# Windowed attention with sink keys before a routed expert: the attention rebuilt around cast loads, key blocks and packed sinks

## The chip, the cores and the metric

The kernel runs on 1 core of one Trainium2 chip. The metric is the device time of one execution in microseconds, the median of the runs; lower is better. The profile is one execution taken by the hardware profiler. PE is TensorE's matmul side and PEld its weight loads; DVE is VectorE, ACT ScalarE, POOL GpSimd, SP SyncE.

## The reference

Four batches, eight heads, 768 positions, head size 64. Each query sees the first four keys (the sinks) and the last 128 keys up to itself:

```
scores = (q @ k.T) / 8;  keep = (key < 4) | (0 <= query - key < 128)
a = softmax(where(keep, scores, -1e9));  x = a @ v          # heads side by side: x is [4, 768, 512]
```

Then, for each batch, a routed expert works on the 128 rows of x with the highest score:

```
s = x @ w_gate;  top = the 128 rows with the largest s
out = x;  out[top] += sigmoid(s[top]) * (relu(x[top] @ w1) @ w2)     # w1 is 512 x 1024, w2 1024 x 512
```

## The kernel before

The work goes batch by batch, and in a batch by six query blocks of 128. A framework takes the program's operations and sets the order on each engine when the kernel is built; the engines then work through fixed lists, and each instruction waits for the semaphores that its operands need. Score tiles turn through two PSUM banks, value tiles through three, everything of the expert through three more.

`prep` (L111 to L169) loads q, k and v of a batch in float32 by SP's queue in 256 KB pieces, whose rows are 256 bytes long (L120, L124, L129), and the four sink rows of v (L134). DVE and ACT cast q and k to bf16 (L139, L140), TensorE transposes two heads at a time (L149), and DVE copies the results out: keys as 128 rows that hold two heads (`KT`, L160), queries into `QTz`, where the rows of the other head are zero (L155, L157, the zeros by POOL at L143). So one score matmul uses all 128 rows of the array though a head has 64.

`stage_scores` makes, per query block, head and visible key block, a 128x128 score tile (L193), adds the mask by a matmul of an identity with a mask of 512 columns (L195) and takes the exponential on ACT (L198). From block 2 on a third set of score matmuls against key block 0 serves the sinks (L209, L213). `stage_av` multiplies the exponentials (as weights, float32) by v: 128 moving columns per head, of which 64 are v, one is a column of ones that gives the softmax's sum, and the rest is not used (L227); the sinks need another matmul per head with a `vsk` that is zero outside four rows (L231). DVE divides (L237, L238), computes the row's routing score (L243), a diagonal of it (`dg`, L249), and a float32 matmul with ones spreads it over all partitions (L253, L260).

`moe_gen` is the expert of the batch before, run in pieces between the query blocks: DVE ranks the rows by counting larger scores (`cjunk`, L283), makes a one-hot matrix per 128 rows (`E`, L286) and its transpose (`ET`), TensorE gathers (L298), multiplies by w1 (L315) and w2 (L322), scatters (L328); DVE adds x (`o_sb`, L331), and SP stores. The last batch's expert has nothing beside it.

Of the kernel before, what the change touches and what calls it, by code (L numbers as in the profile page):

```python
# [9 lines left out]
FP32 = mybir.dt.float32  # L10
# [4 lines left out]
B = 4  # L15
H = 8
# [6 lines left out]
CAP = 128  # L23
MASK_NEG = -30000.0
VSTRIDE = 66
VWIDTH = H * VSTRIDE + 62
# [3 lines left out]
def kernel(  # L30
# [17 lines left out]
    qk32 = ctx.enter_context(tc.tile_pool(name="qk32", bufs=1))  # L48
    vpool = ctx.enter_context(tc.tile_pool(name="vpool", bufs=2))
    qkb = ctx.enter_context(tc.tile_pool(name="qkb", bufs=1))  # L50
    tpool = ctx.enter_context(tc.tile_pool(name="tpool", bufs=2))
    ptpool = ctx.enter_context(tc.tile_pool(name="ptpool", bufs=2))
    xnpool = ctx.enter_context(tc.tile_pool(name="xnpool", bufs=2))
    opool = ctx.enter_context(tc.tile_pool(name="opool", bufs=3))
    mpool = ctx.enter_context(tc.tile_pool(name="mpool", bufs=1))
    spool = ctx.enter_context(tc.tile_pool(name="spool", bufs=2))
# [20 lines left out]
    nc.vector.tensor_copy(maskA0[:], maskB_f[:])  # L77
    maskD_f = cp.tile([128, 128], FP32, name="maskD_f", tag="maskD_f")
    nc.gpsimd.memset(maskD_f[:], 0.0)
    nc.gpsimd.affine_select(  # L80
        out=maskD_f[:], in_=maskD_f[:], compare_op=ALU.is_ge,
        fill=MASK_NEG, base=-1, pattern=[[-1, 128]], channel_multiplier=1,
    )
    maskD = cp.tile([128, 128], BF16, name="maskD", tag="maskD")
    nc.vector.tensor_copy(maskD[:], maskD_f[:])
    nc.gpsimd.memset(maskD_f[0:4, :], 0.0)
    maskC = cp.tile([128, 128], BF16, name="maskC", tag="maskC")
    nc.vector.tensor_copy(maskC[:], maskD_f[:])

    mask4 = {}  # L90
    for mname, mt in (("A0", maskA0), ("B", maskB), ("C", maskC), ("D", maskD)):
        m4 = cp.tile([128, 4, 128], BF16, name=f"mask4{mname}", tag=f"mask4{mname}")
        nc.vector.tensor_copy(out=m4[:, :, :], in_=mt[:, :].unsqueeze(1).to_broadcast((128, 4, 128)))  # L93
        mask4[mname] = m4
# [5 lines left out]

    wgb = cp.tile([128, DM], FP32, name="wgb", tag="wgb")
    nc.gpsimd.dma_start(out=wgb[:], in_=moe_w_gate.partition_broadcast(128))

    ones_f = cp.tile([128, 128], FP32, name="ones_f", tag="ones_f")
    nc.gpsimd.memset(ones_f[:], 1.0)


    class BatchState:
        pass

    def prep(b, first):  # L111
        st = BatchState()
        st.b = b
        qf = qk32.tile([128, NB, H, D], FP32, name="qf", tag="qf")
        kf = qk32.tile([128, NB, H, D], FP32, name="kf", tag="kf")
        vn = vpool.tile([128, NB, VWIDTH], FP32, name="vn", tag="vn")
        nc.gpsimd.memset(vn[:, :, :], 1.0)  # L117
        for c in range(NB):
            tsl = slice(c * 128, (c + 1) * 128)
            nc.sync.dma_start(out=qf[:, c, :, :],  # L120
                              in_=q[b, :, tsl, :].rearrange("h p d -> p h d"))
        for c in range(NB):
            tsl = slice(c * 128, (c + 1) * 128)
            nc.sync.dma_start(out=kf[:, c, :, :],  # L124
                              in_=k[b, :, tsl, :].rearrange("h p d -> p h d"))
        for c in range(NB):
            tsl = slice(c * 128, (c + 1) * 128)
            vdst = vn[:, c, 0:H * VSTRIDE].rearrange("p (h cc) -> p h cc", cc=VSTRIDE)[:, :, 0:D]
            nc.sync.dma_start(out=vdst, in_=v[b, :, tsl, :].rearrange("h p d -> p h d"))  # L129
        vsk = vpool.tile([128, H, 128], FP32, name="vsk", tag="vsk")  # L130
        nc.gpsimd.memset(vsk[:, :, :], 0.0)
        nc.gpsimd.memset(vsk[0:4, :, D:D + 1], 1.0)
        for h in range(H):
            nc.sync.dma_start(out=vsk[0:4, h, 0:D], in_=v[b, h, 0:4, :])  # L134

        qb = qkb.tile([128, NB, H, D], BF16, name="qb", tag="qb")
        kb = qkb.tile([128, NB, H, D], BF16, name="kb", tag="kb")
# [264 lines left out]
```

## Time and profile before

| | |
|---|---|
| runs | 286.36, 287.98, 288.23 us (median 287.98) |
| profiled execution, first to last instruction | 286.7 us |
| PE busy | 224.2 us (78%), 2096 matmul records |
| PEld busy | 194.5 us (68%) |
| DVE busy | 159.2 us (56%) |
| ACT busy | 107.9 us (38%) |
| POOL busy | 41.4 us (14%) |
| chain that ended last | PE 59%, DVE 30%, ACT 4%, DMA 3% |
| DMA | 27.88 MB in 80262 packets, 75568 of them under 512 bytes |

The profile gives the span of one execution; what lies around it is not in it, and the median stands 1.3 us above the span. A busy matmul engine is not one at its peak, since the records of neighbouring matmuls overlap: the distance from one start to the next tells more than the length of a record. A float32 matmul is two records (two passes), each with its own weight load.

### The profile page before, as it was taken

The numbers are of one execution on the slowest core, as the hardware profiler recorded it, in microseconds if no ns is written. First come the engines' busy times: TensorE is split into PE (matmuls) and PEld (weight loads), VectorE is DVE, ScalarE is ACT, GpSimd is POOL, SyncE is SP. The second block draws the span as 40 slices with busy tenths as digits, with TensorE's granted clock in tenths as the row PEclk, the third lists the DMA queues.
The fourth block names the chain that finished last, engine by engine and source line by source line (L and its number), as shares of the span: only waits on it lengthen the run. The fifth ranks groups of instructions, "written<-read, shape, count | busy, mean of one in ns | idle before, by whom it ended". The sixth has DMA issues, their size and how long they took to land.

```text
span 286.7 us, 5137 instructions
## 1 busy us (share of the span) xinstructions
PE 224.2 (78%) x2096; PEld 194.5 (68%) x2096; DVE 159.2 (56%) x366; ACT 107.9 (38%) x205; POOL 41.4 (14%) x33
## 2 busy tenths in 40 slices
PE   0100389948998889999976999999969999997671
PEld 0000268926898779889973799899838899994350
DVE  0799853484039498742469557233695332158814
ACT  0050037042752472376343431851534534424040
POOL 3599200000015500000650000000000000000000
PEclk9999999975999999999999899999997999999597
DMA  7999989979901097910024620000005000000415
GB/s 162 217 219 196 193 159 194 221 134 229 172 0 33 15 213 159 228 21 2 0 59 91 220 77 0 2 2 0 2 11 211 2 0 2 2 0 2 171 49 220
DMA packets 80262, 27.88 MB, mean 97 GB/s; under 512 B 75568, under 2 KB 76592, under 8 KB 80240
## 3 DMA queue, kind: packets, MB, share of 16 engines
q1 hardware_dynamic: 78592, 25.21, 41.5%
q0 software_dynamic: 1648, 2.36, 4.5%
q8 instruction: 16, 0.26, 0.4%
q14 instruction: 6, 0.05, 0.1%
HBM read 23.36 MB, written 6.29 MB: 103 GB/s over the span
## 4 chain that ended last, share of the span: by engine, by line
PE 59%; DVE 30%; ACT 4%; DMA 3%; issue 2%; SPq 0%; ACTq 0%; DVEq 0%
PE xg L227 25%; PE xg L231 9%; DVE cjunk L283 7%; PE sc L193 6%; PE sc L195 5%; PE trp L149 4%; DVE maskA L77 4%; DVE mask4D L93 3%; PE sk L209 3%; ACT pt L198 3%; DMA qf<-in_q_dram 2%; DVE qb L139 2%; DVE junk L243 2%; DVE o_sb L331 2%; DVE E L286 2%
## 5 line engine op out<-in xcount | busy, mean ns | idle before, releaser
L227 PE MATMUL xg<-vn,pt 128*128 128x128 f32 x704 | 110.4, 281 | 0.0
L227 PEld LDWEIGHTS xg<-vn,pt 128*128 128x128 f32 x704 | 96.7, 195 | 1.6 <-issue 0.6
L198 ACT ACTIVATE pt<-sc 128x512 f32<-128x512 f32 x88 | 50.1, 596 | 77.4 <-PE sc L195 76.8
L237 DVE RECIPROCAL rz<-xg 128x4 f32<-128x4 f32 x48 | 8.7, 182 | 93.9 <-PE xg L231 73.4
L231 PE MATMUL xg<-vsk,psk 128*128 128x128 f32 x256 | 50.1, 278 | 0.0
L193 PEld LDWEIGHTS <-KT 128*128 128x128 bf16 x352 | 28.5, 102 | 17.1 <-issue 13.2
L231 PEld LDWEIGHTS xg<-vsk,psk 128*128 128x128 f32 x256 | 39.6, 192 | 0.3
L193 PE MATMUL sc<-QTz,KT 128*128 128x128 bf16 x352 | 36.5, 227 | 1.8 <-ACT pt L198 0.9
L149 PE MATMUL trp<-ident_b,qb 128*128 128x128 bf16 x96 | 9.9, 253 | 34.6 <-DVE qb L139 21.8
L247 ACT CAST xb<-xn 128x512 bf16<-128x512 f32 x24 | 14.8, 616 | 56.5 <-DVE xn L238 56.5
L143 POOL MEMSET QTz<- 128x6144 bf16 x4 | 20.9, 5222 | 89.9 <-PE sk L209 89.9
L149 PEld LDWEIGHTS <-qb 128*128 128x128 bf16 x96 | 7.3, 112 | 36.1 <-DVE qb L139 32.1
L283 DVE TENSOR_SCALAR_CACHE_REDUCE cjunk<-sbc,scol 128x768 f32<-128x768 f32 x24 | 24.2, 1007 | 2.3 <-ACT sbc L263 2.3
L238 DVE TENSOR_TENSOR xn<-xg,rz 128x256 f32<-128x256 f32 x48 | 20.3, 423 | 2.2
L331 DVE TENSOR_TENSOR o_sb<-ops,xb 128x512 f32<-128x512 f32 x24 | 15.7, 682 | 6.6 <-PE ops L328 4.6
L213 ACT ACTIVATE psk<-sk 128x512 f32<-128x512 f32 x32 | 18.2, 599 | 0.5 <-PE sk L209 0.2
L328 PE MATMUL ops<-gye,ET 128*128 128x512 bf16 x24 | 9.3, 443 | 10.1 <-DVE o_sb L331 8.6
L243 DVE CUSTOM_DVE_ANT_0 junk<-xn,wgb 128x512 f32<-128x512 f32 x24 | 16.5, 686 | 0.4
L195 PE MATMUL sc<-mask4B,ident_b 128*128 128x512 bf16 x40 | 16.2, 404 | 0.0
L139 DVE TENSOR_SCALAR qb<-qf 128x1536 bf16<-128x1536 f32 x8 | 10.7, 1338 | 8.9 <-DMA qf<-in_q_dram 8.9
L117 POOL MEMSET vn<- 128x3540 f32 x4 | 12.2, 3052 | 9.3 <-PE xg L227 9.3
L209 PE MATMUL sk<-QTz,KT 128*128 128x128 bf16 x128 | 12.3, 218 | 0.5
(70 smaller groups left out, 255.3 us busy)
## 6 DMA issues: line engine op xcount, KB each, us to landing
qf<-in_q_dram SPq DMA_DIRECT2D x24, 256.0 KB
kf<-in_k_dram SPq DMA_DIRECT2D x24, 256.0 KB
vn<-in_v_dram SPq DMA_DIRECT2D x24, 256.0 KB
out_dram<-o_sb SPq DMA_DIRECT2D x24, 256.0 KB
w_sb<-in_moe_w_dram POOLq DMA_DIRECT2D x2, 1024.0 KB, 12.4
vsk<-in_v_dram SPq DMA_DIRECT2D x32, 1.0 KB
wgb<-in_moe_w_gate_dram POOLq DMA_DIRECT2D x1, 256.0 KB, 5.8
```

What stands on the lines that cost most here:

```text
L143: nc.gpsimd.memset(QTz[:, :, :], 0.0)
L149: nc.tensor.transpose(out=trp[:, c, :], in_=src[:, c, 2 * hp:2 * hp + 2, :], identity=ident_b[:],)
L193: nc.tensor.matmul(out=sc[:, hh, :], lhsT=kt_ap, rhs=qblk, start=(hh == 0), stop=False)
L195: nc.tensor.matmul(out=sc[:, :, :], lhsT=ident_b[:, :], rhs=m4[:, :, :], start=False, stop=True)
L198: nc.scalar.activation(out=pt[:, quad * 4:quad * 4 + 4, :], in_=sc[:, :, :], func=ACT.Exp)
L209: nc.tensor.matmul(out=sk[:, hh, :], lhsT=st.KT[:, hpi, 0:128], rhs=qblk, start=True, stop=True)
L227: nc.tensor.matmul(out=xg[:, hh, :], lhsT=pt_tiles[ci][:, h, :], rhs=vap, start=(ci == 0), stop=(ci == nterm - 1))
L231: nc.tensor.matmul(out=xg[:, hh, :], lhsT=psk[:, h, :], rhs=st.vsk[:, h, :], start=False, stop=True)
L238: nc.vector.tensor_tensor(out=xn32[:, g * 4:(g + 1) * 4, :], in0=xg[:, :, 0:D], in1=rz[:, :, :].to_broadcast((128, 4, D)), op=ALU.mult)
L243: nc.vector.tensor_tensor_reduce(out=junk[:, :], in0=xn_flat, in1=wgb[:, :], scale=1.0, scalar=0.0, op0=ALU.mult, op1=ALU.add, accum_out=s ...
L283: nc.vector.tensor_scalar(out=cjunk[:, :], in0=sbc[:, :], scalar1=scol[:, c:c + 1], scalar2=0.0, op0=ALU.is_gt, op1=ALU.add, accum_out=ran ...
L331: nc.vector.tensor_tensor(out=o_sb[:, :], in0=ops[:, :], in1=xb16[:, c, :], op=ALU.add)
```

## The change

q and k are loaded by POOL's queue and cast to bf16 on the way, with a position's number split as 6 x p + c, so that a partition gets six neighbouring rows of 64 numbers, 1536 bytes in DRAM. Batch 0 comes in four parts each of two heads, later batches in one piece for q and one for k. The transposes take one head at a time (a 64-column tile of the array), and the copies out of PSUM put the positions back in order: keys by DVE, queries by ACT. The zero-padded queries and their zeros are gone.

Scores are made per key block: one matmul of 64 array rows covers a head's key block and the 256 queries that see it (its own block and the next). Only key block 0 keeps the added mask, over four matmuls of 512 columns per batch. For the other blocks POOL zeroes the triangles in the exponentials with two `affine_select` of 128x512 per half of the heads, 18 per batch and 72 in all. The sinks of all heads are packed into one 128-row weight (`ksk`), 32 rows of scores and one matmul per half with v's sink rows (260 columns). The value matmul has 65 moving columns instead of 128. The expert is computed as before, with its pieces cut and its PSUM shared differently: two banks of scores, two value tiles of two banks each, two banks for transposes, sinks and expert together.

```diff
-    x_ps = ctx.enter_context(tc.tile_pool(name="x_ps", bufs=3, space=bass.MemoryType.PSUM))
-    mo_ps = ctx.enter_context(tc.tile_pool(name="mo_ps", bufs=3, space=bass.MemoryType.PSUM))
+    x_ps = ctx.enter_context(tc.tile_pool(name="x_ps", bufs=2, space=bass.MemoryType.PSUM))
+    mo_ps = ctx.enter_context(tc.tile_pool(name="mo_ps", bufs=2, space=bass.MemoryType.PSUM))
...
+    def load_qk(b, parts):
...
+        n = H // parts
+        for i in range(parts):
+            hs = slice(i * n, (i + 1) * n)
+            for src, dst in ((q, st.qb), (k, st.kb)):
+                nc.gpsimd.dma_start(
+                    out=dst[:, hs, :, :].rearrange("p h c d -> p h (c d)"),
+                    in_=src[b, hs, :, :].rearrange("h (p c) d -> p h (c d)", c=NB))
...
+    def transposes(st, hp):
...
+        for src, dst, eng in ((st.kb, st.KT, "v"), (st.qb, st.QT, "s")):
+            trp = mo_ps.tile([128, NB, 128], BF16, name="trp", tag="mo")
+            for c in range(NB):
+                for e in range(2):
+                    nc.tensor.transpose(out=trp[64 * e:64 * e + 64, c, :], in_=src[:, 2 * hp + e, c, :],
+                                        identity=ident_b[:])
+            o = dst[:, hp, :].rearrange("d (p c) -> d p c", c=NB)
+            i = trp[:, :, :].rearrange("d c p -> d p c")
+            if eng == "v":
+                nc.vector.tensor_copy(out=o, in_=i)
+            else:
+                nc.scalar.copy(out=o, in_=i)
...
-                nc.tensor.matmul(out=sc[:, :, :], lhsT=ident_b[:, :],
-                                 rhs=m4[:, :, :], start=False, stop=True)
+    def scores(st, kc, g):
+        nq = 256 if kc + 1 < NB else 128
...
+        banks = [sc_ps.tile([128, 2, 256], FP32, name="sc", tag="sc") for _ in range(2)]
+        for hh in range(2):
+            for e in range(2):
+                hp = 2 * g + hh
+                nc.tensor.matmul(
+                    out=banks[e][:, hh, 0:nq],
+                    lhsT=st.KT[64 * e:64 * e + 64, hp, kc * 128:(kc + 1) * 128],
+                    rhs=st.QT[64 * e:64 * e + 64, hp, kc * 128:kc * 128 + nq],
+                    start=(hh == 0), stop=(hh == 1 and kc > 0), skip_group_check=True)
...
+            nc.scalar.activation(out=po[:, e, :, 0:nq], in_=banks[e][:, :, 0:nq],
+                                 func=ACT.Exp, scale=0.125)
+        if kc > 0:
+            hs = slice(4 * g, 4 * g + 4)
+            nc.gpsimd.affine_select(
+                out=pt[:, hs, 0:128], in_=pt[:, hs, 0:128], compare_op=ALU.is_ge,
+                fill=0.0, base=0, pattern=[[0, 4], [1, 128]], channel_multiplier=-1)
...
+    def pv(st, j, g):
...
+        if j >= 2:
+            nc.tensor.matmul(out=xg[:, g, 0:4 * VS], lhsT=st.psk[:, (j - 2) * 128:(j - 1) * 128],
+                             rhs=st.vsk[:, 4 * g:4 * g + 4, :].rearrange("p h e -> p (h e)"),
+                             start=True, stop=False, skip_group_check=True)
...
+                nc.tensor.matmul(out=xg[:, g, hh * VS:(hh + 1) * VS],
+                                 lhsT=st.pt[kc][:, h, off:off + 128],
+                                 rhs=st.v[:, kc, h, :], start=first, stop=(hh == 3 and kc == j),
+                                 skip_group_check=True)
...
+        if j == 0 and b + 1 < B:
+            states[b + 1] = load_qk(b + 1, 1)
+            load_v(states[b + 1])
...
+        if b + 1 < B and 1 <= j <= HP:
+            transposes(states[b + 1], j - 1)
```

Three places of the new order bear on the prediction. POOL's list at the start, where a DMA row stands for one load that POOL issues; `w_sb` are w1 and w2, and the first `qb` and `kb` of eight heads are those of batch 1:

```order
L122 AFFINE_SELECT m0f<-m0f 128x128
L129 IOTA iota_i 128x128
L322 DMA w_sb<-in_moe_w_dram 128x4x1024 [waits DMASW0_49]
L323 DMA w_sb<-in_moe_w_dram 128x8x512 [waits DMASW1_49]
L77 DMA qb<-in_q_dram 128x8x384 [waits DMASW2_49]
L77 DMA kb<-in_k_dram 128x8x384 [waits DMASW3_49]
```

Batch 1's q and k stand behind both weights in the one queue that casts; before, they came by SP's queue and the weights by POOL's.

PE's list in the first blocks of batch 0 (`kb_318` are batch 1's keys, `xg_382` is the value tile of block 1, `xg_458` that of block 2):

```order
L206 MATMUL xg_458<-vsk0_96,psk_287 128x260 [waits DMAHW2_49,DMAHW3_49,DMAHW1_49,DMAHW4_49,DVE_49,Pool_49]
L170 LDWEIGHTS KT_163
L170 MATMUL sc_373<-QT_162,KT_163 128x256 [waits Activation_49]
L170 LDWEIGHTS KT_163
L170 MATMUL sc_373<-QT_162,KT_163 128x256
L147 LDWEIGHTS kb_318 [waits DMASW3_49]
L147 MATMUL trp_417<-ident_b_115,kb_318 64x128
...
L214 MATMUL xg_382<-vbuf0_94,pt_335 128x65 [waits DMAHW1_49,Pool_49]
```

The transposes of batch 1's keys, which wait for their load, now stand ahead of nearly all value matmuls of batch 0 (nine of 88 are in front of them).

PE's list in a block of batch 1: scores of 64 array rows (L170), value matmuls (L214), expert (L263):

```order
L170 LDWEIGHTS KT_416
L170 MATMUL sc_852<-QT_415,KT_416 128x256 [waits Activation_49]
L170 LDWEIGHTS KT_416
L170 MATMUL sc_852<-QT_415,KT_416 128x256
L214 MATMUL xg_827<-vbuf1_95,pt_683 128x65
L214 MATMUL xg_827<-vbuf1_95,pt_747 128x65 [waits Pool_49]
L214 MATMUL xg_827<-vbuf1_95,pt_683 128x65
L263 LDWEIGHTS E_802 [waits DVE_49]
L263 MATMUL etp_842<-ident_b_115,E_802 128x128
L170 LDWEIGHTS KT_416
L170 MATMUL sc_853<-QT_415,KT_416 128x256 [waits Activation_49]
```

Rows of 64-row tiles and of the whole array follow one another in short runs; with the 64-column transposes the tile changes 150 times in the program, where before it never did.

## Rows read from the trace of the kernel before

**Rows 1.** Windows: start to batch 0's first transposes, four ends of value matmuls, rest.

```profile
core 0: us, PE busy (x) PEld busy (x) DVE busy (x) ACT busy (x) POOL busy (x), PEclk, DMA share, GB/s
0.00:32.20 32.20, 0.80 (x6) 0.63 (x6) 23.28 (x12) 4.23 (x3) 22.67 (x25) 1.00 1.06 198
32.20:96.10 63.90, 55.65 (x489) 48.38 (x490) 31.49 (x67) 24.20 (x39) 5.73 (x2) 0.92 0.77 140
96.10:145.00 48.90, 46.07 (x454) 42.12 (x453) 29.76 (x82) 24.67 (x41) 9.34 (x5) 1.00 0.50 93
145.00:203.10 58.10, 53.70 (x523) 47.18 (x521) 31.95 (x87) 23.73 (x49) 3.63 (x3) 0.97 0.21 55
203.10:256.30 53.20, 50.17 (x479) 44.81 (x476) 24.61 (x75) 23.64 (x49) 0.00 (x0) 0.97 0.08 31
256.30:286.70 30.40, 17.83 (x160) 11.41 (x157) 18.12 (x46) 7.43 (x24) 0.00 (x0) 0.83 0.28 104
```

**Rows 2.** The chain of waits at the start: start, length, what (us).

```profile
10.60 9.48 DVE mask4D L93
20.07 10.68 DVE maskA L77
```

**Rows 3.** DVE and POOL groups by line: busy us, mean ns; then DVE in order of time.

```profile
L93 DVE COPY mask4B<-maskB 128x512 bf16<-128x512 bf16 x1 | 0.3, 304 | 0.0
L80 POOL TENSOR_SCALAR_AFFINE_SELECT maskD_f<-maskD_f 128x128 f32<-128x128 f32 x1 | 0.3, 290 | 0.0
L105 POOL MEMSET ones_f<- 128x128 f32 x1 | 0.2, 194 | 0.0
L131 POOL MEMSET vsk<- 128x1024 f32 x4 | 4.0, 1000 | 0.0
...
92.24 0.29 DVE L249 TENSOR_SCALAR dg<-ident_f,scol 128x128 f32<-128x128 f32 x1
97.19 1.52 DVE L249 TENSOR_SCALAR dg<-ident_f,scol 128x128 f32<-128x128 f32 x1
```

**Rows 4.** PE in order of time: streamed float32 passes, then a pair after idle time.

```profile
247.01 0.61 PE L227 MATMUL xg<-vn,pt 128*128 128x128 f32 x4
247.45 0.39 PE L231 MATMUL xg<-vsk,psk 128*128 128x128 f32 x2
247.68 0.61 PE L227 MATMUL xg<-vn,pt 128*128 128x128 f32 x4
98.77 0.49 PE L260 MATMUL bcB<-dg,ones_f 128*128 128x128 f32 x2 [1.01 <-DVE scol L294]
```

**Rows 5.** The chain of waits later on: bf16 matmuls of 128 and of 512 columns.

```profile
110.09 0.67 PE trp L149 x12
275.88 1.74 PE yeps L322 x8
```

**Rows 6.** PE groups by line: records, busy us, mean ns of one.

```profile
L227 PE MATMUL xg<-vn,pt 128*128 128x128 f32 x704 | 110.4, 281 | 0.0
L231 PE MATMUL xg<-vsk,psk 128*128 128x128 f32 x256 | 50.1, 278 | 0.0
```

**Rows 7.** The weights' loads by POOL's queue, two issues; then windows of loading.

```profile
DMA to landing us min/median/max: 9.4/12.4/15.4
...
24.00:28.00 4.00, 0.00 (x0) 0.00 (x0) 4.00 (x2) 0.00 (x0) 4.00 (x3) 1.00 1.12 201
39.00:44.00 5.00, 4.92 (x43) 3.86 (x43) 1.08 (x2) 3.11 (x6) 0.00 (x0) 1.00 1.24 232
```

**Rows 8.** The chain of waits at the end: start, length, what (us).

```profile
256.04 0.24 PE xg L231 x2
265.31 0.88 issue
266.27 0.61 DVE o_sb L331
270.33 2.73 PE xeT L298 x24
```

**Rows 9.** Groups by line: ACT's exponentials and POOL's issue of a load.

```profile
L198 ACT ACTIVATE pt<-sc 128x512 f32<-128x512 f32 x88 | 50.1, 596 | 77.4 <-PE sc L195 76.8
L340 POOL DMA_DIRECT2D w_sb<-in_moe_w_dram x1 | 0.7, 747 | 0.0
```

More of the change, by code (lines that the diff above doesn't have):

```diff
@@ L77 @@
[L77 to L94, printed above, removed]
+    for i in range(2):
+        nc.vector.memset(vsk[i][:, :, :], 0.0)
+        nc.vector.memset(ksk[i][:, :, :], 0.0)
+        nc.vector.memset(vbuf[i][:, :, :, D:D + 1], 1.0)
@@ L273, in moe_gen @@
     def moe_gen(st):
         b = st.b
-        scol, xb16 = st.scol, st.xb16
-        sbc = st.sbc
+        scol = st.scol
+        sbc = mp.tile([128, S], FP32, name="sbc", tag="sbc")
+        for half in range(2):
+            bc = mo_ps.tile([128, 3, 128], FP32, name="bc", tag="mo")
+            for jj in range(3):
+                j = 3 * half + jj
+                dg = sp.tile([128, 128], FP32, name="dg", tag="dg")
+                nc.vector.tensor_scalar_mul(out=dg[:, :], in0=ident_f[:, :], scalar1=scol[:, j:j + 1])
+                nc.tensor.matmul(out=bc[:, jj, :], lhsT=ones_f[:, :], rhs=dg[:, :],
+                                 start=True, stop=True)
+            nc.scalar.copy(out=sbc[:, 384 * half:384 * half + 384],
+                           in_=bc[:, :, :].rearrange("p a n -> p (a n)"))
@@ L310, in moe_gen @@
         nc.vector.reciprocal(out=gt[:, :], in_=gt[:, :])
-        hT_sb = mpool.tile([128, 8, 128], BF16, name="hT_sb", tag="hT_sb")
-        for fc in range(8):
-            hps = mo_ps.tile([128, DM], FP32, name="hps", tag="big")
-            for dc in range(4):
-                nc.tensor.matmul(out=hps[:, 0:128],
-                                 lhsT=w1_sb[:, dc, fc * 128:(fc + 1) * 128],
-                                 rhs=xeT_sb[:, dc, :], start=(dc == 0), stop=(dc == 3))
-            nc.scalar.activation(out=hT_sb[:, fc, :], in_=hps[:, 0:128], func=ACT.Relu)
@@ L335 @@
-    PREP_AT = 2
-    MOE_AT = 2
-    states = {}
-    states[0] = prep(0, first=True)
-    w1_sb = wp.tile([128, 4, FF], BF16, name="w1_sb", tag="w1_sb")
+        yield
+        hT = mp.tile([128, 8, 128], BF16, name="hT", tag="hT")
+        for fq in range(2):
+            hps = mo_ps.tile([128, 4, 128], FP32, name="hps", tag="mo")
+            for f4 in range(4):
+                fc = 4 * fq + f4
+                for dc in range(4):
+                    nc.tensor.matmul(out=hps[:, f4, :], lhsT=w1_sb[:, dc, fc * 128:(fc + 1) * 128],
+                                     rhs=xeT_sb[:, dc, :], start=(dc == 0), stop=(dc == 3))
+            nc.scalar.activation(out=hT[:, 4 * fq:4 * fq + 4, :], in_=hps[:, :, :], func=ACT.Relu)
+            yield
@@ L340, with start_state @@
+    def start_state(st):
+        st.pt = {}
+        st.x = xp.tile([128, NB, DM], FP32, name="x", tag="x")
+        st.xb = xp.tile([128, NB, DM], BF16, name="xb", tag="xb")
+        st.scol = sp.tile([128, NB], FP32, name="scol", tag="scol")
+    states = {0: st0}
+    for hp in range(HP):
+        transposes(st0, hp)
+    start_state(st0)
+    sink_scores(st0)
     nc.gpsimd.dma_start(out=w1_sb[:], in_=moe_w1.rearrange("(dc p) f -> p dc f", p=128))
-    w2_sb = wp.tile([128, 8, DM], BF16, name="w2_sb", tag="w2_sb")
```

373 lines of the change are left out of this document (148 added, 225 removed).

## The prediction

> **What bounds the kernel now.** I read the windows first [rows 1]. Between the first value matmuls and the last, TensorE is nearly full: batches 1 to 3 take 48.9 + 58.1 + 53.2 = 160.2 us and PE is busy for 149.9 of them, 6.4% idle. DVE has 25 to 32 us of work in each, ACT 24, POOL under 10. So the middle is paid in PE time. The two ends are not: 32.2 us pass before the first transposes run on, and 30.4 us after the last value matmul. In the chain of waits the start is two DVE copies of 9.48 and 10.68 us [rows 2], of a kind that takes 304 ns otherwise [rows 3]; POOL has its memsets back to back all that time. A `dg` takes 0.29 us alone and 1.52 us beside a memset [rows 3]. So a DVE copy or scaling between SBUF tiles waits until POOL pauses.
>
> In order of time, float32 value matmuls run at a beat: three per head, six records, 0.67 us apart from head to head (247.01 to 247.68), so 0.112 us per pass and 0.223 us per matmul [rows 4]. The 704 + 256 records [rows 6] are 480 such matmuls, 107 us of PE's time. A bf16 matmul of 128 columns takes 0.67 / 12 = 0.056 us, one of 512 columns 1.74 / 8 = 0.217 us [rows 5].
>
> **What the beat of 0.112 us is.** It decides most of this change. A pair of passes in the stream lasts 0.39 us, a pair after idle time 0.49 us [rows 4]. The 0.10 us more is the load of 128 float32 weights, which in the stream hides behind the pass before. Load (0.10) and 128 columns (0.112) are about equally long. With 65 columns the moving part falls to 0.112 x 65/128 = 0.057 us, but the weights are still 128 columns of float32. So I keep 0.112 us per pass: narrower value matmuls gain nothing, fewer of them do. The other end is 0.057.
>
> **The start.** The DVE copies of 20 us are gone: masks are built with short POOL work, and there is no padding to zero. POOL issues eight loads at about 0.75 us each [rows 9], batch 0's transposes follow the parts as they land, and the first exponentials should stand near 20 us. But PE's list then has the transposes of batch 1's keys, and these wait for a load that is last of twelve in POOL's queue, behind 1.57 MB of batch 0's q and k, 2.1 MB of weights and 0.79 MB of batch 1's q; with itself 5.24 MB as written. The weights alone, 2.1 MB, landed 15.4 us after their issue [rows 7], about 14 us of moving, which is 150 GB/s: 5.24 MB take 35 us, so 37 with a 2 us start, and 34 as the lower end if batch 0's parts move faster than the weights did. SP's v loads share the DMA engines: with them 6.8 to 8.4 MB at 201 to 232 GB/s [rows 7] take 29 to 42 us, 44 with the start, and 46 as the upper end. I take **43 us**, near the upper end, since v's loads stand in SP's queue from the start and the 14 us were measured with little beside them. The routing weights stand behind batch 0's v in SP's queue, so DVE's first routing score waits about as long; PE needs nothing from it sooner. Up to there PE has done the 96 transposes of batch 0, 19 score matmuls and nine value matmuls.
>
> **From there to the last value matmul**, PE's work:
> - value: 352 - 9 = 343 matmuls x 0.223 = 76.5 us. Before, 480 in all; the 128 sink matmuls go.
> - packed sinks: 31 of 260 columns, two passes of 0.112 x 260/128 = 0.227: 14.0 us.
> - scores: 141 of 256 columns (0.112) and 32 of 128 (0.056) are 17.6 us one after another, 8.8 if two 64-row tiles run side by side. Before no tile was smaller than the array; I take the middle, 13.2.
> - masks and sink scores: 24 of 512 columns, 5.2 us; before, 88 mask matmuls alone were 19 us.
> - transposes of batches 1 to 3: 288 x 0.056 = 16.1 us, 8.1 side by side; 12.1.
> - the expert of batches 0 to 2, as before: per batch six float32 matmuls (1.34), 68 bf16 of 128 columns or fewer (3.8), 14 of 512 (3.04): 8.2, so 24.6 us.
>
> Together 145.6 us (137.2 to 154). To it come about 131 changes of tile in this stretch. No row has one. Nothing is the lower end; the upper is a pipe that empties: the record of a streamed pass outlasts its beat by 0.39 - 2 x 0.112 = 0.165 us, and the next load is no longer hidden, 0.10: 0.265 us each, 35 us in all. I take 0.10, the exposed load alone, since that is the one price here that a row shows by itself: 13.1 us. Idle time was 6.4%; I take 10% (up to 15), because the expert, the transposes and the sinks now share two PSUM banks where the expert had three and DVE's strided copy holds one longer. (145.6 + 13.1) / 0.9 = **176 us**.
>
> One rule speaks against the tiles. A restart after idle time costs a float32 pair 0.10 us [rows 4], and no row has a change of tile. The Trainium skill, TensorEngine Tiling (Array Packing), Key Properties, says that changing the tiling mode (not just the tile) drains TensorE. By the row the forecast stays 247 us; by the rule it would be case 2 below, 271 us. No run here shows yet which holds.
>
> **What lies beside it.** POOL's 72 masks: a 128x128 one took 290 ns, and memsets grow by (1000 - 194) / 896 = 0.9 ns per element [rows 3], so 512 columns take between 0.29 + 0.34 = 0.63 and 4 x 0.29 = 1.16 us. At 0.85 that is 3.4 us per block of about 8, and they are asked for one block before their value matmul. The exponentials keep their 0.6 us per 512 columns [rows 9]: 25 of them per batch instead of 30, hidden behind the value matmuls of a half block (four heads, 1.8 us). DVE loses the casts and the padded copies, and gains copies with a stride; its 25 to 32 us per batch stay about 30. These cost nothing as long as PE has 45 us or more per batch. If the cover goes, the order in which they come to light is DVE, then ACT.
>
> **The end.** From 256.3 on [rows 1, 8] the chain is division, routing score, six rankings, then the last batch's expert. Between 265.31 and 270.33 it stood in outputs of the batch before [rows 8]; the new pieces are done by then, so 5.0 us go, of which about 0.6 come back (the six transposes of `E`). One wide division instead of two halves and a Relu of 512 columns add about 0.8: 30.4 - 3.8 = **26.6 us** (25.5 to 29).
>
> Sum: 43 + 176 + 26.6 = 245.6 us against the profiled span of 286.7. The median of the runs stands 1.3 us above that span, so **247 us** is forecast against 287.98.
>
> **The cases.**
> 1. As above, 50%: 232 to 262 us, with the landing between 36 and 46 and the tile price between 0.05 and 0.17.
> 2. Every tile change empties the pipe, 22%. It is the rule of the Trainium skill named above; the price is from rows. For it: a pair after idle time does pay its load [rows 4]. Against: in the stream the load is hidden behind a pass of any other tensor. 131 x 0.165 / 0.9 = 24 us more: 271 us.
> 3. Value matmuls do get shorter with their columns, 15%. For it: the load's record could include a fixed part that overlaps. Against: the 0.10 us of [rows 4]. 343 x 2 x 0.055 = 37.7 us less PE time, (145.6 - 37.7 + 13.1) / 0.85 = 142 us with DVE now close behind: 213 us.
> 4. Keys of batch 1 land early and tiles cost nothing while pairs overlap, 8%: 34 + 137.2 / 0.936 + 26.6 + 1.3 = 208 us at the extreme, 228 half way from there to case 1.
> 5. Slower, 5%: POOL's masks lock DVE. Per batch 14 DVE instructions (six `dg`, six `E`, two casts or scalings) are of the kind that waited in [rows 3]. If each waits for a whole block's run of four masks, 3.4 us, DVE has 30 + 48 = 78 us per batch and bounds it: 78 us for batch 0 + 3 x 78 + 26.6, about 339 us. It decides from a mean wait of (63 - 30) / 14 = 2.4 us, where a batch takes 63 us and all that is gained is given back. Against: the masks come in pairs with exponentials between, so a run is rather 1.7 us.
>
> That the change does not do what it says could only be the pairing; without it 8.4 / 0.9 = 9 us more, inside case 1.
>
> The range 212 to 276 takes cases 1, 2 and 4, and half of case 3. About 1% (2.9 us) can be told from no change. Faster by more: 94%, all but case 5 and the far end of case 2; within 1%: 2%; slower: 4%.
>
> **What would show it.** The distance between value passes: 0.112 us, or 0.06. The first transposes of batch 1 starting at once after their load lands, near 43 us, with PE idle from about 25 us. The start of the first value pass after a score matmul: 0.05 to 0.1 us later than in the stream, or 0.27. Score matmuls of two row halves starting a few ns or 0.11 us apart. Masks near 0.85 us. `dg` and `E` with a mean below 0.7 us. From the last value matmul to the end 26 to 27 us. The forecast is wrong if PE's beat in the values changes, or if another engine has the longer list in batches 1 and 2.

## The result, and the profile after

The changed kernel takes 240.0 us (median of 4 runs, 236.7 to 248.4) against 287.5 us of the kernel before on the same chip: ratio 0.826, 95% interval 0.821 to 0.830. The forecast was 247 us, the range 212 to 276. The profiled execution's span is 236.3 us, its time 238.0. The ratio rests on the two runs of 236.7 and 238.0 us; the other two, 242.0 and 248.4, were disturbed ones with a lower granted clock.

The page of the changed kernel, in its own rows: span, busy time of the engines, PE's busy tenths and granted clock in 40 slices, and the chain that ended last.

```profile
span 236.3 us, 4345 instructions
PE 196.0 (83%) x1752; PEld 154.7 (65%) x1752; DVE 118.5 (50%) x292; ACT 90.4 (38%) x169; POOL 59.1 (25%) x101
...
PE   0369701999999999999999999999999999944850
...
PEclk9999955555699999999999999999999999985595
...
PE 74%; DMA 13%; DVE 5%; POOL 4%; issue 1%; ACT 1%; POOLq 0%; DVEq 0%
```

PE bounds it in the middle, as before. Two things are new: an empty stretch near 30 us, and six slices at half clock behind it (before, batch 0 had a clock of 0.92 on the mean [rows 1], which is some 10 us at half clock). The windows show them by stage (columns as in [rows 1]).

```profile
core 0: us, PE busy (x) PEld busy (x) DVE busy (x) ACT busy (x) POOL busy (x), PEclk, DMA share, GB/s
...
28.50:40.40 11.90, 0.01 (x1) 0.00 (x0) 0.00 (x0) 0.64 (x2) 1.62 (x3) 0.55 1.27 203
40.40:63.70 23.30, 23.25 (x134) 19.13 (x135) 6.67 (x18) 6.86 (x12) 4.49 (x7) 0.50 0.85 145
63.70:83.30 19.60, 19.57 (x194) 16.20 (x194) 6.48 (x17) 8.68 (x18) 5.48 (x8) 1.00 0.55 90
...
126.90:170.60 43.70, 43.70 (x440) 35.35 (x440) 29.26 (x71) 22.18 (x43) 11.13 (x18) 1.00 0.15 48
...
206.30:236.30 30.00, 13.96 (x94) 8.98 (x93) 14.51 (x36) 4.02 (x8) 0.00 (x0) 0.68 0.14 54
```

From 28.5 to 40.4 us PE has nothing; then it is busy without a gap, but for 23.3 us at a granted clock of 0.50, which is 1.2 of its 2.4 GHz. A batch at full clock takes 43.7 us, all of it PE; before it was 48.9 to 58.1 [rows 1]. DVE has 29 us in it and POOL 11. The time came out of the batches: the last value matmul of batch 0 starts at 81.7 us (before, batch 0 ended at 96.1), that of batch 3 at 205.9 (256.3). So 14 us of the 50 lie in the start and batch 0, 36 in batches 1 to 3, 0.4 in the end, where 3.8 were forecast.

The chain of waits at the start (start, us, what):

```profile
11.40 29.01 DMA kb<-in_k_dram
40.41 0.04 issue
40.45 0.95 PE trp L147 x13
41.41 0.54 PE sc L170 x2
```

The place is the forecast one, the keys of batch 1; [rows 2] had two DVE copies here. The order of time on PE in the middle (start, us, op, count):

```profile
119.80 1.03 PE L196 MATMUL sk<-QT,ksk 128*128 128x512 bf16 x4
120.67 1.90 PE L214 MATMUL xg<-vbuf,pt 128*128 128x65 f32 x16
122.49 0.39 PE L170 MATMUL sc<-QT,KT 64*128 64x256 bf16 x4
122.82 0.39 PE L177 MATMUL sc<-mask,ident_b 128*128 128x512 bf16 x1
```

Sixteen value passes of 65 columns from 120.67 to 122.49 are 0.114 us apart (0.112 within the run): the beat of [rows 4], where they had 128 columns. Four score matmuls of 256 columns on 64 rows take 0.33 us from start to start of what follows, though one alone is 0.107 us of columns at 2.4 GHz, four 0.43: pairs run side by side (the two halves' records start 3 ns apart).

The groups that answer to [rows 3]:

```profile
L184 POOL TENSOR_SCALAR_AFFINE_SELECT pt<-pt 128x512 f32<-128x512 f32 x40 | 25.6, 641 | 131.8 <-ACT pt L180 131.8
L243 DVE TENSOR_SCALAR dg<-ident_f,scol 128x128 f32<-128x128 f32 x24 | 9.8, 422 | 0.8 <-PE bc L244 0.5
L257 DVE TENSOR_SCALAR E<-iota_f,rank 128x128 bf16<-128x128 f32 x24 | 8.8, 365 | 0.2
```

A mask takes 0.64 us; `dg`, beside masks, 0.42 on the mean. The chain at the end:

```profile
217.69 2.03 PE xeT L271 x19
...
220.74 3.57 PE hps L290 x32
224.31 1.74 PE ye L296 x8
...
227.95 2.02 DMA out_dram<-o_sb
```

`hps` took 2.10 us before; here it begins at half clock.

### The profile page after: what moved, and what is told of

It reads as the page before. It is cut to its first block, busy times and chain, and to the rows that moved or that the text cites. A ratio compares the mean times of both kernels' runs of the same rounds, so it can differ in the third digit from the quotient of the medians.

```text
span 236.3 us, 4345 instructions
## 1 busy us (share of the span) xinstructions
PE 196.0 (83%) x1752; PEld 154.7 (65%) x1752; DVE 118.5 (50%) x292; ACT 90.4 (38%) x169; POOL 59.1 (25%) x101
## 4 chain that ended last, share of the span: by engine, by line
PE 74%; DMA 13%; DVE 5%; POOL 4%; issue 1%; ACT 1%; POOLq 0%; DVEq 0%
PE xg L214 36%; DMA kb<-in_k_dram 12%; PE xg L206 8%; PE sc L170 7%; PE trp L147 5%; PE hps L290 4%; PE ye L296 3%; PE bc L244 3%; PE xeT L271 3%; DVE cjunk L254 2%; PE ops L303 2%; PE sc L177 1%; POOL qb L77 1%; POOL kb L77 1%; PE sk L196 1%; DVE o_sb L305 1%
## 5 line engine op out<-in xcount | busy, mean ns | idle before, releaser
L214 PEld LDWEIGHTS xg<-vbuf,pt 128*128 128x128 f32 x704 | 92.9, 205 | 8.6 <-issue 5.4
L214 PE MATMUL xg<-vbuf,pt 128*128 128x65 f32 x704 | 96.7, 289 | 0.0
L180 ACT ACTIVATE pt<-sc 128x512 f32<-128x512 f32 (+1 forms) x96 | 50.3, 562 | 53.6 <-PE sc L170 47.2
L184 POOL TENSOR_SCALAR_AFFINE_SELECT pt<-pt 128x512 f32<-128x512 f32 x40 | 25.6, 641 | 131.8 <-ACT pt L180 131.8
L154 ACT COPY QT<-trp 128x768 bf16<-128x768 bf16 x16 | 12.8, 802 | 32.8 <-PE trp L147 32.8
L170 PE MATMUL sc<-QT,KT 64*128 64x256 bf16 (+1 forms) x192 | 24.3, 281 | 0.7 <-ACT pt L180 0.7
L228 DVE CUSTOM_DVE_ANT_0 junk<-x,wgb 128x512 f32<-128x512 f32 x24 | 16.5, 687 | 14.7 <-DMA wgb<-in_moe_w_gate_dram 14.4
L206 PE MATMUL xg<-vsk,psk 128*128 128x260 f32 x64 | 22.5, 435 | 0.0
L305 DVE TENSOR_TENSOR o_sb<-ops,x 128x512 f32<-128x512 f32 x24 | 15.7, 688 | 10.9 <-PE ops L303 9.5
L188 POOL TENSOR_SCALAR_AFFINE_SELECT pt<-pt 128x512 f32<-128x512 f32 x32 | 20.3, 634 | 0.0
L225 DVE TENSOR_TENSOR x<-xg,rz 128x512 f32<-128x512 f32 x24 | 16.5, 686 | 0.4
L206 PEld LDWEIGHTS xg<-vsk,psk 128*128 128x128 f32 x64 | 10.7, 196 | 5.0 <-issue 2.5
L170 PEld LDWEIGHTS <-KT 64*128 64x128 bf16 x192 | 7.1, 95 | 10.4 <-issue 6.6
L263 PE MATMUL etp<-ident_b,E 128*128 128x128 bf16 x24 | 5.7, 237 | 6.2 <-DVE E L257 6.2
```

The source lines that it names most:

```text
L170: nc.tensor.matmul(out=banks[e][:, hh, 0:nq], lhsT=st.KT[64 * e:64 * e + 64, hp, kc * 128:(kc + 1) * 128], rhs=st.QT[64 * e:64 * e + 64, h ...
L180: nc.scalar.activation(out=po[:, e, :, 0:nq], in_=banks[e][:, :, 0:nq], func=ACT.Exp, scale=0.125)
L184: nc.gpsimd.affine_select(out=pt[:, hs, 0:128], in_=pt[:, hs, 0:128], compare_op=ALU.is_ge, fill=0.0, base=0, pattern=[[0, 4], [1, 128]], ...
L188: nc.gpsimd.affine_select(out=pt[:, hs, 128:256], in_=pt[:, hs, 128:256], compare_op=ALU.is_ge, fill=0.0, base=-1, pattern=[[0, 4], [-1, 1 ...
L206: nc.tensor.matmul(out=xg[:, g, 0:4 * VS], lhsT=st.psk[:, (j - 2) * 128:(j - 1) * 128], rhs=st.vsk[:, 4 * g:4 * g + 4, :].rearrange("p h e ...
L214: nc.tensor.matmul(out=xg[:, g, hh * VS:(hh + 1) * VS], lhsT=st.pt[kc][:, h, off:off + 128], rhs=st.v[:, kc, h, :], start=first, stop=(hh ...
```

## The experiments

In all of them the kernel before ran on the same chip, and ratios are to it. Where a kernel is built on another, the diff is against that one. Diffs are shortened, `...` marks what is left out. An edit can also change the order that the framework gives PE's list; where it did, the text says so.

**Early keys.** Is the landing's price only the wait?

```diff
-    nc.gpsimd.dma_start(out=w1_sb[:], ...)      # ahead of the loop
-    nc.gpsimd.dma_start(out=w2_sb[:], ...)
             states[b + 1] = load_qk(b + 1, 1)
+            if b == 0:
+                nc.gpsimd.dma_start(out=w1_sb[:], ...)
+                nc.gpsimd.dma_start(out=w2_sb[:], ...)
```

> Only the order of POOL's loads is changed: q and k of batch 1 are issued ahead of the two expert weights. Theory (the load of batch 1's keys costs twice: 12 us in which TensorE stands still, and then a stretch of 22.6 us at a granted clock of 0.50, in which twice the time is spent): by bytes the keys land after 3.15 of the 5.24 MB that POOL loads, near 25 us and not at 40.4, TensorE gets there at about 28, there is no long wait and the clock stays at 1.0; 12 + 11 = 23 us less, about 217 us, and the stretch from 28 to 60 shows the clock at 1.0. Rival A (the clock falls whatever is done, the wait alone goes): 12 us less, 228 us, with the clock still at 0.50 near 40 to 60. Rival B (the DMA engines as a whole set the landing, since v of batches 0 and 1 moves beside it, or the routing weights, which land at 41.5 us, hold DVE and then TensorE): the wait moves to another place, 236 to 240 us.

Measured: 241.3, 241.6 and 242.5 us, and 229.7 in a fourth run; whether it is faster than the changed kernel stays open. In the profiled run (241.6) PE waited only 3.7 us, up to 27.3 instead of 40.4. The window behind it:

```profile
27.60:78.80 51.20, 51.20 (x286) 40.10 (x286) 13.13 (x34) 16.17 (x30) 13.76 (x21) 0.50 0.76 131
```

The wait went, and the stretch at half clock grew from 34 us (of which PE worked 23.3) to 51, with PE busy in all of it. The clock fell all the same, as in rival A, whose 228 us the fourth run comes near; how long it stays down was in no theory, and it differs from run to run. The mean granted clock was 0.898 in the fourth run and 0.843 to 0.856 in the others: 23 us of the span lost against 35 to 38, about the difference in time.

**Early keys and early routing weights.** The load of `wgb` moved ahead of `load_v(st0)` on SP.

> As the kernel in which q and k of batch 1 are issued ahead of the expert weights, and in addition SP issues the routing weights ahead of batch 0's values (they landed at 41.5 us and DVE waited 14.4 us for them). Theory (TensorE does not need DVE's first routing score for two blocks): the same time as with the q and k order alone within 1%, about 217 us, with DVE's wait gone. Rival (once the keys are early, the routing weights are what holds the value tiles): 3 to 10 us faster than with the q and k order alone. Second rival: the broadcast of the routing weights delays batch 0's values and TensorE's first value matmul, 1 to 2 us slower.

Measured: 235.3 us, ratio to before 0.816 (0.810 to 0.822). The timeline of PE (idle time in brackets) and the window behind:

```profile
26.73 0.42 PE L147 MATMUL trp<-ident_b,kb 128*64 128x128 bf16 x3 [4.32 <-DMA kb<-in_k_dram]
```

```profile
25.50:66.50 41.00, 39.77 (x220) 31.22 (x220) 11.03 (x27) 13.12 (x24) 10.71 (x17) 0.50 0.98 164
```

DVE's wait for the routing weights is gone. The stretch at half clock is 10 us shorter than in the profiled run above, which is worth 5 of the 7 us between the two profiled spans (233.0 and 239.9). But the fourth run above was faster than any here, so what the routing weights give by themselves stays open.

**Tile changes doubled.** Scores and values of a half block interleaved in two pieces:

```diff
-                scores(states[nxt[0]], nxt[1], g)
-            pv(st, j, g)
+            sg, pg = scores(...), pv(st, j, g)      # each yields after half of its matmuls
+            next(sg); next(pg); next(sg, None); next(pg, None)
```

> The score matmuls of a half block are issued in two pairs, each ahead of two heads of value matmuls, instead of all four ahead of four heads: the same work, but 120 more changes of tile size on TensorE (270 instead of 150). Theory (a change costs the 0.10 us of the load that is no longer hidden): 120 x 0.10 = 12 us more, 252 us. Rival A (the pipe runs empty and a change costs 0.265 us): 32 us more, 272 us. Rival B (a change costs nothing, the extra distance seen is that of starting another accumulation): 240 us, within 1%.

Measured: 263.9 us, 0.915 (0.908 to 0.921), between theory and rival A. The window at half clock, and that of one batch at full clock, tell the parts:

```profile
26.70:88.20 61.50, 48.93 (x270) 39.73 (x271) 12.31 (x32) 12.33 (x22) 10.24 (x16) 0.50 0.63 110
...
142.30:190.20 47.90, 47.90 (x440) 37.57 (x440) 28.84 (x70) 22.66 (x43) 11.12 (x18) 1.00 0.14 45
```

A batch is 47.9 instead of 43.7 us, with 73 changes instead of 39 in it: 4.2 / 34 = **0.124 us per change**, 120 of them 14.9 us. The half-clock stretch is 61.5 instead of 34 us long; PE works 48.9 us in it instead of 23.3, and half of the difference, 12.8 us, more than makes up the rest. An empty pipe at 0.265 us is out, and so is a change that costs nothing.

**Value matmuls of 112 columns.**

```diff
-vp.tile([128, NB, H, VS], FP32, ...)       # 65 columns, the last of ones
+vp.tile([128, NB, H, 112], FP32, ...)      # 112, the last 48 of ones
```

> The value matmuls get 112 columns instead of 65 (64 values, then 48 columns of ones instead of one); everything else the same, but for about 5 us of memset on DVE in the first 10 us. Theory (the beat of 0.112 us per pass is the load of 128 float32 weights, the columns pass beside it): the beat stays 0.112 us, 238 to 243 us in all. Rival (the columns are the beat, at 0.84 ns each for float32): 704 passes x 47 x 0.84 ns = 28 us more where the load does not cover them, up to 268 us.

Measured: 240.4 us (240.2 to 240.5), 0.834 (0.830 to 0.839): the total agrees with the theory, but by two effects that cancel.

```profile
29.20:49.70 20.50, 9.82 (x58) 8.10 (x59) 2.71 (x8) 1.19 (x2) 2.41 (x4) 0.50 1.27 209
...
121.50:167.80 46.30, 45.16 (x441) 35.31 (x439) 27.43 (x70) 22.34 (x42) 11.16 (x18) 1.00 0.15 47
```

In the stream passes still start 0.112 us apart. A batch takes 2.6 us more; by columns alone it would be 7. Of the 2.6, PE stands still for 1.1, and about 0.8 are columns that show at the first pass of a run (0.096 or 0.200 us to the next start, with 65 columns 0.057 or 0.161; some 20 runs per batch). And the clock was back 9.8 us after the keys, not 23.3.

**A filler in the wait.** 55 matmuls into a tile that nobody reads, ahead of batch 1's transposes:

```diff
+        if b == 0 and j == 1:
+            dmy = mo_ps.tile([128, 512], FP32, name="dmy", tag="mo")
+            for _ in range(55):
+                nc.tensor.matmul(out=dmy[:, :], lhsT=ident_b[:, :], rhs=mask0 (512 columns),
+                                 start=True, stop=True)
         if b + 1 < B and 1 <= j <= HP:
             transposes(states[b + 1], j - 1)
```

> The changed kernel with 55 matmuls of 512 bfloat16 columns added (a mask times the identity, into a PSUM tile that nobody reads), 47 of them directly ahead of the transposes of batch 1, where TensorE waited 12 us for the keys: 47 x 0.217 = 10.2 us of work in the wait. Loads stay in their order, so the landing near 40 us stays. Theory (the wait itself is not the only cost; the clock falls because TensorE stands still, and stays at 0.50 for 23 us of work behind it): the clock stays at 1.0, the keys land at 40 as before, and 23.3 / 2 = 11.5 us are gained behind the wait: 226 to 229 us against 238 to 242. Rival A (the fall has nothing to do with the wait: value matmuls of 65 columns keep the clock down in any case): clock at 0.50 from about 27 to 60 as before, 238 to 242 us. Rival B (the wait alone costs, the clock makes no difference since something else sets the pace behind it): the clock at 1.0 and still 238 to 242 us.

Measured: 227.1 us (226.6 to 227.7), 0.788 (0.786 to 0.791).

```profile
33.00:43.30 10.30, 10.30 (x51) 4.56 (x50) 1.04 (x4) 0.00 (x0) 1.03 (x2) 1.00 1.29 209
43.30:69.40 26.10, 26.07 (x280) 21.86 (x280) 10.76 (x29) 13.29 (x25) 7.91 (x12) 1.00 0.87 159
```

```profile
31.20 2.00 PE L214 MATMUL xg<-vbuf,pt 128*128 128x65 f32 x16
33.04 10.31 PE L349 MATMUL dmy<-mask,ident_b 128*128 128x512 bf16 x47
```

The transposes start no earlier (43.3 us), loads are as they were, and the time is as the theory has it. Added work that does nothing makes the kernel faster than the changed one, by 0.788 / 0.826 = 0.955 (0.946 to 0.963 from the ends of the two intervals), some 11 us.

Not all of that is the clock. With the filler PE's list also has 15 more value matmuls and four more score matmuls ahead of batch 1's transposes (48 value passes instead of 18). Between the landing and the end of batch 0's window, 42.9 us became 26.1: 11.7 by the clock (half of 23.3) and about 5 by work that moved elsewhere. Against it, the transposes start 2.9 us later, behind the filler, and the stretch of the last batch is 2.7 us longer (38.4 for 35.7).

**Both.** Early keys, early routing weights and 22 such matmuls.

> The kernel with q and k of batch 1 ahead of the expert weights and the routing weights ahead of batch 0's values (234.7 us, its clock at 0.50 from 25.5 to 66.5 us), with 22 matmuls of 512 columns that nobody reads, 14 of them directly ahead of batch 1's transposes, where it waited 4.3 us. Theory (the early keys gained little because the clock, once it had fallen in that short wait, stayed down for 41 us): the clock stays at 1.0 and half of 41 us is gained: 214 us (212 to 217). Rival A (the clock stays down with narrow value matmuls whatever fills the wait): 233 to 236 us. Rival B (the clock holds, but then loads of v or of the weights are late): a new wait ahead of 60 us, 218 to 228 us.

Measured: 218.1 us (215.7 to 219.9), 0.759 (0.753 to 0.765); the profiled run 215.7. The clock is 1.0 from the first transposes of batch 1 on, which start at 33.5 us:

```profile
33.50:59.60 26.10, 26.07 (x280) 21.84 (x280) 9.11 (x24) 12.79 (x24) 7.92 (x12) 1.00 1.18 188
```

The same 26.1 us as in the kernel above, with the same work ahead of the transposes, and no new wait behind them. So the early keys are worth about 10 us, once the clock holds: the transposes start at 33.5 us instead of 43.3.

**bfloat16 exponentials and values**, on the kernel with both:

```diff
-st.pt[kc] = pp.tile([128, H, 256], FP32, ...);  vbuf, vsk, psk FP32;  v loaded by SP
+st.pt[kc] = pp.tile([128, H, 256], BF16, ...);  vbuf, vsk, psk BF16;  v cast on load, by POOL
```

> The kernel with early keys and the filler ahead of batch 1's transposes, and exponentials, sink exponentials and values in bfloat16 (v by cast loads from POOL's queue): value matmuls of one pass instead of two, with a bfloat16 load. Theory (a value matmul's 0.223 us is two loads of 128 float32 columns): the beat is that of the bfloat16 matmuls with 128 columns of weights, 0.056 us; per batch TensorE saves 88 x 0.167 = 14.7 us and 8 packed sinks x 0.33 = 2.6 us of 43.6 and is no longer the bound; DVE's 29 us are: 30 to 33 us per batch, about 165 to 180 us in all. Rival (the load takes as long in bfloat16, only the second pass goes): a beat of 0.112 us, 31 us per batch on TensorE itself, 170 to 182 us; the beat tells the two apart, not the time. Rival B (waits for PSUM and POOL, hidden now under TensorE's 43.6 us, come to light): over 185 us.

Measured: 195.5 us (190.7 to 202.5; the profiled run 195.4). In its timeline and on its page:

```profile
117.02 0.41 PE L215 MATMUL xg<-vbuf,pt 128*128 128x65 bf16 x8
117.26 0.27 PE L207 MATMUL xg<-vsk,psk 128*128 128x260 bf16 x1
```

```profile
PEclk9999999556985579995795569999855798555596
```

Eight value matmuls in 0.24 us, 0.030 each, where float32 takes 0.223: shorter than both beats expected. 65 columns at 2.4 GHz are 0.027 us, so the load of bfloat16 weights hides even behind these. The Trainium skill, TensorE: Matmul & The Clock Gate, Weight-path perf modes, says that the fast weight load is for 128 weights of a type other than float32; the two beats agree with it in direction. The time is rival B's, with another reason: the clock falls again and again, for 86 of the profiled run's 194 us.

**Without the masks**, one look (the affine_selects of L184 and L188 left out):

> The changed kernel without the 72 triangle masks on GpSimd (the exponentials outside the window are then summed too). Theory (the masks are hidden: they stand one block ahead of their use): the batches keep their pitch of 43.6 us to within 0.3 us from last value matmul to last value matmul; on DVE `dg` falls from 0.47 to 0.29 us and `E` from 0.39 to 0.29, the rows that shared the port with the masks. Rival A (a mask is the last thing that the first value matmul of a block waits for): pitch shorter by 1 us or more per batch. Rival B (GpSimd does not hold DVE up, `dg` is slower for another reason): `dg` stays at 0.4 us or more.

```profile
117.40:160.60 43.20, 43.20 (x441) 35.17 (x439) 26.80 (x70) 22.14 (x42) 0.00 (x0) 1.00 0.16 50
```

```profile
L234 DVE TENSOR_SCALAR dg<-ident_f,scol 128x128 f32<-128x128 f32 x24 | 6.4, 285 | 2.6 <-PE bc L235 2.5
```

The one run took 230.1 us, with a half-clock stretch of 27 us and again 48 value passes ahead of batch 1's transposes, so the batch decides. It is about 0.45 us shorter, a little over the theory's bound; `dg` is back at 0.285 us and `E` at 0.276. POOL's masks do hold such DVE instructions up, by 0.14 us at a time, and PE's 43.7 us hide it.

The start of this run also bears on the clock:

```profile
22.30:29.10 6.80, 6.80 (x47) 4.93 (x47) 0.90 (x2) 5.10 (x10) 0.00 (x0) 1.00 1.23 194
29.10:33.50 4.40, 4.40 (x20) 3.31 (x19) 0.00 (x0) 0.81 (x2) 0.00 (x0) 0.50 1.27 191
33.50:40.10 6.60, 0.03 (x1) 0.00 (x0) 0.00 (x0) 0.60 (x1) 0.00 (x0) 0.50 1.26 211
```

The clock fell at 29.1 us, while PE was busy without a gap by its records (two mask matmuls of 512 columns, then scores and value matmuls of 65), 4.4 us before its wait for the keys began. So the clock can fall ahead of the wait. The filler above may have held it by its eight matmuls among the first scores and value matmuls, by the 47 in the wait, or by both; that the wait is what made it fall is not shown.

**Sinks apart**, on the kernel with early keys and filler: four matmuls of 65 columns in place of one of 260.

```diff
-nc.tensor.matmul(out=xg[:, g, 0:4 * VS], lhsT=st.psk[...], rhs=st.vsk[:, 4 * g:4 * g + 4, :] ...)
+for hh in range(4):
+    nc.tensor.matmul(out=xg[:, g, hh * VS:(hh + 1) * VS], lhsT=st.psk[...], rhs=st.vsk[:, 4 * g + hh, :] ...)
```

> The kernel with early keys and the filler (216 to 220 us, clock at 1.0), with one part of the change undone: the sinks of four heads are added by four float32 matmuls of 65 columns instead of one of 260, with the same weights and the same 260 columns in all: 128 matmuls instead of 32. Theory (a float32 pass never takes less than the 0.112 us of its load): four matmuls take 8 x 0.112 = 0.89 us, one takes 2 x 0.219 = 0.44; 32 half blocks x 0.46 = 14.6 us more, 231 us (229 to 234). Rival (columns are what counts, at 0.84 ns): no change, 216 to 220 us. Second rival (each matmul costs more than its loads, 0.30 us with some start of its own): over 240 us.

Measured: 233.3 us, 0.808 (0.803 to 0.814), 15.2 us above its base from median to median (14.6 expected), though on another chip. One batch:

```profile
115.00:162.00 47.00, 46.79 (x486) 39.70 (x486) 29.48 (x70) 21.97 (x42) 11.13 (x18) 1.00 0.15 46
```

The base has 43.7 us, so eight half blocks take 3.3 us more, 0.41 each instead of the 0.46 expected, and 32 of them 13.2 us; the profiled run also started batch 1's transposes 3.8 us later (37.3 us), so that the total came so near is partly luck. The same weights and columns with four times the passes: at 65 columns a float32 value matmul costs its passes and not its columns. That the load is what fills a pass fits the bfloat16 beat; no run changes the columns of float32 weights alone.

**A filler in the last ranking**, on the same base: 12 matmuls behind the routing scores, four behind each of five rankings.

> The kernel with early keys and the filler (216 to 220 us), with 32 matmuls of 512 columns that nobody reads in the last batch's ranking: 12 behind the routing scores and four behind each of the first five rankings. There the clock fell to 0.50 for 13.7 us, and the last expert ran in it. Theory (the clock fell because TensorE waits for DVE's rankings): the clock stays at 1.0, gathering and both expert products, 2.2 + 3.2 + 1.9 us, take 1.5 + 2.1 + 1.7: from the last value matmul to the end 28 us instead of 30.0, and the time 2 us less, 214 to 218 us. Rival A (DVE's rankings and the copies between the products set the end, not TensorE): 30 us from the last value matmul to the end. Rival B (the fillers stand in front of the transposes of the rankings and delay them): more than 30 us.

Measured: 215.7 us, 0.751 (0.745 to 0.757), against 0.759 (0.753 to 0.765): the totals can't be told apart. The last window, and `hps` in the chain of waits:

```profile
184.50:213.10 28.60, 17.78 (x127) 9.36 (x128) 14.57 (x36) 4.01 (x8) 0.00 (x0) 0.88 0.15 56
```

```profile
198.88 1.95 PE hps L301 x32
```

28.6 us instead of 30.0, `hps` at 1.95 instead of 3.19: the filler won 1.4 us there, net of four of its own matmuls that stand in the chain with 1.04 us.

**bfloat16 with filler.** Four matmuls of 252 columns per half block into the value tile's unused columns, the filler of the end, six output buffers:

> The kernel with bfloat16 exponentials and values (190.7 to 202.5 us; its clock was at 0.50 for some 95 of 194 us), with filler: four matmuls of 252 columns per half block into the unused columns of the value tile (0.42 us each half block, 5 us per batch), the filler of the last ranking, and six output buffers instead of three. Theory (TensorE is no longer full, the clock falls again and again, and at 0.50 TensorE is the bound once more): with filler the clock stays at 1.0, TensorE has about 29 us per batch and DVE as much, 31 us per batch, 168 to 178 us in all. Rival A (the clock falls all the same, and the filler costs its 5 us per batch, at half clock 10): 200 to 225 us. Rival B (DVE and two PSUM banks set the pace, not the clock): the clock at 1.0 and still 188 to 196 us.

Measured: **177.3 us** (177.0 to 179.4), 0.618 (0.613 to 0.622), the fastest of all.

```profile
PEclk9999999999997869999999999999999999699997
```

```profile
65.60:150.90 85.30, 78.03 (x963) 50.64 (x970) 69.81 (x172) 54.15 (x104) 34.41 (x51) 1.00 0.32 68
```

The clock holds but for a few slices, and 14 us come back from fastest run to fastest run, 18 from median to median, though PE has 192 more matmuls of 252 columns (0.105 us each at 2.4 GHz). What the end and the output buffers have of it is not told apart. PE is busy for 91% and DVE for 82% of this stretch: neither has much left.

**112 columns with early keys, no filler.** Does the clock come back sooner here too?

> The kernel with early keys and early routing weights but without filler (its clock stood at 0.50 from 25.5 to 66.5 us, 41 us, though TensorE was busy in nearly all of it), now with value matmuls of 112 columns instead of 65. Theory (once the clock has fallen, a stream of narrow value matmuls behind long loads keeps it down; with 112 columns the same loads bring it back sooner, as in the changed kernel, where it came back 9.8 us after the keys instead of 23.3): at 0.50 for 10 to 25 us. The wider matmuls cost 2.65 us per batch, as before, and half of 16 to 31 us comes back: 228 to 238 us. Rival (when the clock comes back has nothing to do with the columns): at 0.50 for 35 us or more, 242 to 248 us.

Measured: 225.1 us, 0.781 (0.777 to 0.786), against 235.3 with 65 columns.

```profile
26.40:33.20 6.80, 6.69 (x43) 4.67 (x43) 1.75 (x4) 2.20 (x4) 2.06 (x3) 0.50 1.15 200
```

The stretch at half clock is 6.8 us instead of 41, less than the theory had dared. With 47 columns of ones that nobody needs the kernel is 10 us faster. That the columns alone do it is not shown, since PE's list changed too: six more score matmuls and six more value passes stand ahead of the wait, which is 2.8 instead of 4.3 us long, and in the 6.8 us PE ran transposes and scores for 3.5 us, then 14 value passes.

## Why the prediction was right, and where not

**The beat** was the decisive step, and right: a float32 value pass takes 0.112 us, with 65 columns as with 128 [rows 4, 6]. Case 3 is refuted, by the timeline, by 112 columns in the same stream, and by the sinks taken apart at 0.41 us per half block.

**The start**: the keys landed at 40.4 us for 43 forecast, PE was idle from 28.5 for 25. The first value pass ran at 20.1 us.

**The middle** came out at 165.8 us (40.4 to 206.2) for 176, by terms that erred in both directions. Scores and transposes run side by side, so the lower end of the work, 137.2 us, holds and not 145.6. A change of tile costs 0.124 us and not 0.10: 131 make 16.2. Together 153.4 us. Idle time was put at 10%, 17.6 us: that term failed, the windows have none. And a term was missing: 23.3 us at half clock, 11.7 us lost. 153.4 + 11.7 = 165.1. The forecast foresaw the wait for the keys but gave the clock no term, though [rows 1] has stretches at 0.92 and 0.83; behind the wait it cost as much as the wait.

**The rule on tiles.** Case 2, each change empties the pipe, has failed in its price: the distance after a value pass is 0.208 us before a score tile and 0.112 in the stream (122.285 to 122.493 us), 0.096 more, near the 0.10 forecast. The mean of the doubling is 0.124, since the second value pass behind a change comes late too (0.161 instead of 0.112 us). The Trainium skill, TensorEngine Tiling (Array Packing), Key Properties, says that a change of mode drains TensorE; the trace agrees that a change has a price, below half of the 0.265 us that I had worked out for a drain. Whether it is a drain or the exposed load, no run tells.

**The masks** take 0.64 us, the lower bound, not 0.85. They do hold DVE up, `dg` 0.42 instead of 0.285 us, but by 0.14 and not 3.4 us at a time: case 5 lacked the size, not the mechanism.

**The end** was 30.0 us and not 26.6, outside its range of 25.5 to 29. (The sum in the forecast is off by 0.2: 5.0 - 0.6 - 0.8 is 3.6, not 3.8.) The outputs of the batch before left the chain as forecast, but with 4.1 us and not 5.0. What came back, against 30.4 us before: 1.5 us in `hps` at half clock (the filler in the ranking won 1.4 us in all), 0.7 in the rankings and the first transpose of `E`, 0.8 ahead of them, and 1.2 behind the last `o_sb`; the gathering became 0.4 shorter. The missing term is again the clock, for less than half of the 3.4 us.

So 43 + 176 + 26.6 became 40.4 + 165.8 + 30.0. The mechanism of the middle was right in its beat and its tiles; that the total came within 4% (245.6 against 236.3 us) is in part luck, since 17.6 us of idle time that did not come stood in for 11.7 us of clock that had no term.

Open: why the clock falls at the start, and why it came back after 6.8, 20, 27, 34, 41, 51 or 61 us in different kernels. The account is also that of the profiled executions. Another one of the changed kernel had a mean granted clock of 0.959 instead of 0.888, as high as with the filler in the wait (0.960), and yet took 236.7 us where that kernel took 227.1; one with the tile changes doubled had 0.963 instead of 0.845 and was no shorter. No trace of these two was kept. And no run takes the masks or the pairs of heads back alone, so their shares of the gain are read from the rows, not tested.

## What to carry to other kernels

Find the load behind each matmul before counting its columns: here, with 128 columns of float32 weights, the number of passes was the price up to 128 moving columns, so fewer and wider matmuls paid, and narrower ones did not. A wait on the tensor engine is to be priced with the clock around it, from the granted clock of the windows; where the wait can't go, work that nobody reads may be cheaper than idleness. After an edit, compare the engine's list too: the filler and the wider columns moved work that nobody had asked to move. And check each term against its own stretch: here a forgotten 12 us and an idle share that did not exist hid one another.

## What was not expected of the hardware

- The granted clock fell to 0.50 in a wait of 3 to 14 us or just behind it, and once with PE busy, ahead of the wait. With float32 value matmuls of 65 columns as the main work it then stayed there for 27 to 61 us, PE being busy by its records in all but the wait (a pass takes 0.21 us then). With 112 columns it was back after 9.8 us of work and, in the other kernel, after 6.8 us in all.
- A bfloat16 value matmul of 65 columns takes 0.030 us, 7.4 times less than in float32: one pass instead of two, and no load in sight.
- Two 64-row score matmuls of 256 columns start 3 ns apart, two 64-column transposes 3 to 4 ns.
